# The back half of an attention pipeline moved one tile step later, with a sixth score buffer

## The chip, the cores and the metric

The kernel runs on one NeuronCore of a Trainium2 chip. The metric is the device time in microseconds; the median of the runs is what counts. Engines are named as the profile names them: PE (matmul; PEld its weight loads), DVE (vector), ACT (scalar), POOL (GpSimd), SP (issues most DMAs).

## What is computed

Attention over 4 batches, 8 heads, 576 positions and a head size of 64, in which each query keeps only its 32 largest scores; then a dense two-layer block (512 to 2048 to 512) with a hard-swish between; then a mixture of 8 experts (512 to 1024 to 512), one expert for each of 2304 tokens.

```python
scores = scale * q @ k.T                       # 4 x 8 x 576 x 576
kth = np.partition(scores, -32, axis=-1)[..., -32:-31]
attn = softmax(np.where(scores >= kth, scores, -1e9)) @ v
x = attn.transpose(0, 2, 1, 3).reshape(2304, 512)
h = x @ w_in
x = (h * np.clip(h + 3, 0, 6) / 6) @ w_out     # first block
e = argmax(x @ w_gate); p = softmax(x @ w_gate)[e]
out = p * (relu(x @ w1[e]) @ w2[e])            # experts
```

## The kernel before

**Tiles and steps.** The scores are cut into 144 tiles of 128 query rows by 576 keys (two tiles, one for each head, share a pair of heads; 16 "T" tiles hold the 64-row tails of two heads). One loop with a step counter `t` runs over the tiles (L1102 and below). In step `t` it issues the work of several tiles: scores of tile t+2 (`qk`, `sevac`), first search on tile t (`top_a`: eight MAX8 over pieces of 72, then three rounds that end in the 24 largest), thresholds, exponential and sign count of tile t-1 (`top_c`, `act_exp`, `act_sign`), second search and mask of tile t-2 (`mask`), transposes of tile t-4 (`trans`, `tevac`), the product with v and its way into the input of the first block for tile t-5 (`pv`, `xevac`, `xt`). After these, step `t` issues what the second search needs of tile t-1: the scores with the 24 largest blanked out.

**Second search.** For the first 20 tiles (`ZPE = 20`) POOL writes a mask of large negative numbers into a `z` buffer (L703, `z_pe`), and PE computes the scores a second time on top of that mask in the two PSUM banks `yps2` (`qk(t, zw)`, L630 with output yps), which the first block's second layer is not using yet. From tile 20 on DVE writes the blanked scores into a `z` buffer itself (L696, `top_z`). There are two `z` buffers. In `mask` DVE takes the 8 largest of these (L731), picks the 32nd-largest score with the sign count (`j`, L735, which reads a table in the PSUM tile `ptps`), and multiplies the exponentials by the mask (L739, read from a score buffer). `ptps` is also where the transposes (L755, L757) and the product with v (L789) land.

**Buffers.** Scores: `NSB = 3 + LA` = 5 buffers, tile t in buffer t % 5 (`LA` is 2, the lead of the scores). Exponentials: 3 pair buffers. Query tiles: 2 of each kind (`QB`); `qlast(n)` says in which step the buffer of visit n (4 tiles of a pair of heads) is free again: for the first 20 tiles after the second `qk`.

**First block.** 9 blocks of 256 tokens, 16 groups each, 144 groups. `moe_step` issues one group for each step of the loop as soon as the block's tokens are through `xt` (`blkready`): `l1` (12 matmuls, L863), `epi_a` (ACT, L869), `epi_b` (DVE, L875), `epi_c` (POOL), `l2` (6 matmuls, L894). By the loop's own count block 0 is ready in step 21 and group 0 is issued in step 22, one group a step from then on without a gap; the last step of the loop is 150, with group 128, and the remaining groups follow in a loop without attention. The weights of the first block come as 64-bit numbers and are converted in 32 pieces (`conv64`), 15 in 16 steps, from the start on; a piece has three DVE operations (L329, L336, L339), in `cvs` buffers of which there are three. `gate` transposes the first block's output (`yt`, one buffer) for the expert choice.

**Order.** Every issue sets a due time, `pr(name)`: the step's base plus 400 for each step plus an entry of the table `PRIO` (L50). The framework's scheduler orders each engine's instructions by due time among those whose inputs are already placed, allots buffers, and adds the waits. Engines run their own lists in order. Entries that matter here: `exp=-295, qk=10, pv=-40, top_c=55, mask=55, zw=60, zpe=70, prep=105, sign=175, trans=210, top8=270, l2=260, l1=310, max8=315, z=365, sevac=390, match=560`.

Of the kernel before, what the change touches and what calls it, by code (L numbers as in the profile page):

```python
# [13 lines left out]
F32 = mybir.dt.float32  # L14
# [4 lines left out]
AF = mybir.ActivationFunctionType  # L19
# [11 lines left out]
LA = 2  # L31
# [16 lines left out]
ZPE = 20  # L48
# [9 lines left out]
def attention_two_moe_kernel(  # L58
# [13 lines left out]
    PE, V, A, G, SP = nc.tensor, nc.vector, nc.scalar, nc.gpsimd, nc.sync  # L72
# [5 lines left out]
    P = 128  # L78
# [75 lines left out]
    def pr(name, least=0):  # L154
        tc.cur_priority = max(least, pr0[0] + PRIO[name])
# [72 lines left out]
    def body(cs, exact, ends=None):  # L228
# [160 lines left out]
        if not exact:  # L389
            identb.append(ap1.tile([P, P], BF16, name="identb"))  # L390
            G.tensor_copy(identb[0], ident)
        NPB, NSB, VB = 3, 3 + LA, 2

# [304 lines left out]
        def z_pe(t):  # L698
            if exact or not 0 <= t < ZPE:
                return  # L700
            pr("zw")
            zw = ap1.tile([P, S], F32, tag="z", bufs=2, name=f"z{t}").bitcast(BF16)[:, 0:S]
            G.tensor_scalar(zw, ts[t]["s"][:, 0:S], ts[t]["u"], -HUGE, op0=ALU.is_gt, op1=ALU.mult)  # L703
            qk(t, zw)

# [8 lines left out]
        def act_sign(t):  # L714
            if exact:
                return
            pr("sign")
            d = ts[t]
            jk = ap1.tile([P, S], BF16, tag="jk", bufs=1, name=f"jk{t}")
            d["sg"] = ap1.tile([P, 1], F32, tag="sg", bufs=3, name=f"sg{t}")  # L720
            A.activation(jk, d["s"][:, 0:S], AF.Sign, bias=ts[t]["u"], scale=-1.0, accum_out=d["sg"])  # L721

        def mask(t):
# [3 lines left out]
            if not exact:  # L727
                pr("max8")
                z8 = ap1.tile([P, 8], F32, tag="z8", bufs=3, name=f"z8_{t}")
                j8 = ap1.tile([P, 8, 2], F32, tag="j8", bufs=1, name=f"j8_{t}")  # L730
                V.max(z8, d["z"])  # L731
                A.activation(zall[:, t:t + 1], z8[:, 1:2], AF.Sign, bias=ts[t]["u"], scale=-1.0)
                yield
                pr("match")
                V.scalar_tensor_tensor(j8, psum_isum, d["sg"], z8.unsqueeze(2).to_broadcast([P, 8, 2]), op0=ALU.is_equal, op1=ALU.mult,  # L735
                                       accum_out=tall[:, t:t + 1])
                yield
# [171 lines left out]
        def gate(bk, tt, y):  # L909
            pr("gate")  # L910
            i = bk * (TB // P) + tt
            last = bk == NBLK - 1
            yt = (wp[0] if last else m1p).tile([P, NCC, P], F32, tag="yt", bufs=1 + last, name=f"yt{i}")
            for hf in range(0 if last else 2):
# [186 lines left out]
        cacc = 0  # L1101
        for t in range(T + 7):  # L1102
            pr0[0] = pbase + t * STEP
            loads(t)
            if t == 5:
                load_gates(ts[5]["s"])
            while vloaded[0] < NV and (vloaded[0] < VB or vlast[vloaded[0] - VB] <= t - 6):
                load_v()
            ms = moe_step()
            next(ms, None)  # L1110
            if 0 <= t - 4 < T:
                trans(t - 4)
            if 0 <= t - 1 < T:
                top_c(t - 1)
                act_exp(t - 1)
            if t + LA < T:
                ensure(t + LA)
                qk(t + LA)
            if 0 <= t - 5 < T:
                pv(t - 5)  # L1120
            if t + LA < T:
                sevac(t + LA)
            if 0 <= t - 5 < T:
                xevac(t - 5)
            xg = None
            if xtq and (xtq[0][2] < t - 5 or t >= T):
                xg = xt(*xtq.pop(0))
                next(xg)
            if 0 <= t - 4 < T:
                tevac(t - 4)  # L1130
            if xg:
# [10 lines left out]
            cacc += CRATE  # L1142
            others = [ms, mask(t - 2)]
            while cacc >= 16:
# [315 lines left out]
```

## Time and profile before

| | us |
|---|---|
| median of 3 runs | 1199.18 |
| lowest, highest | 1198.66, 1202.45 |
| the profiled execution | 1204.39 |
| its span from the first to the last instruction | 1202.5 |
| PE, PEld busy | 1118.5, 1003.8 |
| DVE busy | 940.9 |
| ACT busy | 807.6 |
| POOL busy | 458.5 |

The attention loop ends at about 880 us of the span; groups of the first block without attention fill the time to about 930 us; the experts follow. The profile's PE time is modelled: matmuls are pipelined and a busy PE need not be at its peak. Waits are idle times of an engine, put down to the event that ended them.

### The profile page before, as it was taken

To read this page: it belongs to the slowest core of one execution; us is meant where nothing else is said; L and a number is where in the kernel's file an instruction comes from. 1 tells how busy PE (TensorE), PEld (TensorE's weight loads), DVE (VectorE), ACT (ScalarE), POOL (GpSimd) and SP (SyncE) were. 2 spreads that over 40 slices of the span, in tenths; PEclk is the share of its full clock that TensorE was granted. 3 is DMA by queue.
4 is the path that set the end of the run, shared out by engine and by line. 5 is a ranking of instruction groups with operands and counts; after the bars stand their busy time and mean duration, and the time that the engine had idled before them with its cause. 6 is when DMAs were issued, how large, how long until landed. Compare 5 with 4: busy or idle time off the path is not lost.

```text
span 1202.5 us, 24061 instructions
## 1 busy us (share of the span) xinstructions
PE 1118.5 (93%) x7414; PEld 1003.8 (83%) x7414; DVE 940.9 (78%) x3853; ACT 807.6 (67%) x2082; POOL 458.5 (38%) x668
## 2 busy tenths in 40 slices
PE   5677688999999999999999999999999899999995
PEld 4566577778999989999988899999888799888885
DVE  5989989999999999998999899999641554545540
ACT  4777877778878788778778788777541353444441
POOL 5877646644332354433342432322344311222110
PEclk9668879999999999999999999999999899999998
DMA  3654456564553555754444554543486555455530
GB/s 76 189 179 142 143 171 221 162 174 125 157 134 113 151 134 142 177 135 135 118 122 126 133 147 125 152 133 110 127 271 163 176 187 179 161 176 185 160 121 31
DMA packets 184123, 179.24 MB, mean 149 GB/s; under 512 B 123629, under 2 KB 148509, under 8 KB 183984
## 3 DMA queue, kind: packets, MB, share of 16 engines
q1 hardware_dynamic: 178960, 167.24, 48.3%
q0 software_dynamic: 3872, 10.08, 2.6%
q8 instruction: 61, 1.00, 0.4%
q14 instruction: 78, 0.64, 0.2%
q10 hardware_dynamic: 1152, 0.28, 0.1%
HBM read 159.53 MB, written 18.61 MB: 148 GB/s over the span
## 4 chain that ended last, share of the span: by engine, by line
PE 71%; DVE 16%; issue 5%; ACT 4%; POOL 2%; DMA 2%; SPq 0%; POOLq 0%; ACTq 0%; DVEq 0%
PE l1ps L863 15%; PE yps L894 13%; PE ptps L789 9%; PE lp L1263 8%; PE ops L1286 8%; PE sps L630 6%; PE ptps L755 4%; DVE cd L660 2%; DVE pbuf L739 2%; DVE z L696 2%; DVE z L731 1%; PE ptps L935 1%; DVE m L666 1%; DVE cw L671 1%; PE misc L474 1%
## 5 line engine op out<-in xcount | busy, mean ns | idle before, releaser
L894 PE MATMUL yps<-wo,gh 128*128 128x512 f32 x544 | 206.7, 418 | 0.1
L298 POOL TENSOR_SCALAR gh<-gf 128x256 fp32r<-128x256 f32 x144 | 72.7, 505 | 345.2 <-PE yps L894 196.0
L660 DVE MAX8 cd<-sbuf 128x8 f32<-128x72 f32 x1152 | 187.9, 218 | 3.4 <-ACT sbuf L300 3.2
L863 PE MATMUL l1ps<-xh,wih 128*128 128x256 f32 x576 | 167.6, 291 | 4.7 <-DVE gf L875 3.1
L863 PE MATMUL l1ps<-xh,wil 128*128 128x256 f32 x576 | 164.0, 285 | 0.0
L863 PE MATMUL l1ps<-xl,wih 128*128 128x256 f32 x576 | 163.9, 285 | 0.0
L789 PE MATMUL ptps<-vn,pt 128*128 128x65 f32 (+1 forms) x1152 | 145.8, 281 | 0.0
L789 PEld LDWEIGHTS ptps<-vn,pt 128*128 128x128 f32 x1152 | 143.0, 201 | 0.0
L739 DVE SCALAR_TENSOR_TENSOR pbuf<-sbuf,tall,pbuf 128x576 f32<-128x576 f32 x144 | 136.8, 950 | 0.1
L883 POOL TENSOR_TENSOR gl<-gf,gh 128x256 fp32r<-128x256 f32 x144 | 125.5, 871 | 11.4
L863 PEld LDWEIGHTS l1ps<-xh,wih 128*128 128x128 f32 x576 | 110.4, 192 | 14.9 <-DVE gf L875 7.6
L1036 DVE TENSOR_TENSOR wl<-raw,wh 128x1024 fp32r<-128x1024 f32 x64 | 78.6, 1236 | 53.7 <-ACT wh L1035 51.6
L721 ACT ACTIVATE jk<-sbuf,uall 128x576 bf16<-128x576 f32 x144 | 111.6, 775 | 4.2 <-DVE j L735 0.9
L863 PEld LDWEIGHTS l1ps<-xl,wih 128*128 128x128 f32 x576 | 110.6, 192 | 4.2
L712 ACT ACTIVATE pbuf<-sbuf,nb 128x576 f32<-128x576 f32 x144 | 111.2, 775 | 4.1 <-PE ptps L757 0.9
L894 PEld LDWEIGHTS yps<-wo,gh 128*128 128x128 f32 x544 | 101.2, 190 | 14.8 <-POOL qh L486 0.3
L300 ACT ACTIVATE sbuf<-sps 128x576 f32<-128x576 f32 x144 | 92.9, 645 | 30.4 <-PE sps L630 16.5
L869 ACT ACTIVATE gf<-l1ps,three 128x256 f32<-128x256 f32 x144 | 67.9, 471 | 66.9 <-PE l1ps L863 55.7
L755 PE MATMUL ptps<-ident,pbuf 128*128 128x128 f32 x576 | 93.9, 286 | 19.7 <-DVE j L735 12.6
L894 PE MATMUL yps<-wo,gl 128*128 128x512 f32 x272 | 110.4, 406 | 0.6 <-POOL gl L883 0.6
L863 PEld LDWEIGHTS l1ps<-xh,wil 128*128 128x128 f32 x576 | 110.6, 192 | 0.1
L630 PE MATMUL sps<-kx,qh 128*128 128x288 f32 (+2 forms) x336 | 96.8, 319 | 14.3 <-ACT sbuf L300 10.5
(259 smaller groups left out, 2974.7 us busy)
## 6 DMA issues: line engine op xcount, KB each, us to landing
wo<-wod SPq DMA_DIRECT2D x144, 512.0 KB, 3.8
raw<-in_moe_w_dram SPq DMA_DIRECT2D x64, 512.0 KB, 4.3
vn<-in_v_dram SPq DMA_DIRECT2D x96, 128.0 KB, 2.7
rawi<-in_moe_w_in_dram SPq DMA_DIRECT2D x16, 512.0 KB, 4.0
rawo<-in_moe_w_out_dram SPq DMA_DIRECT2D x16, 512.0 KB, 4.6
wod<-wc SPq DMA_DIRECT2D x16, 512.0 KB, 5.6
qn<-in_q_dram SPq DMA_DIRECT2D x126, 64.0 KB, 2.5
yd<-y SPq DMA_DIRECT2D x18, 258.0 KB, 5.1
```

Of the source, the lines that this page charges most:

```text
L630: PE.matmul(d_, a_, b_, start=(i == 0), stop=(i == len(mm) - 1))
L660: V.max(cd[:, c, :], s[:, c * CK:(c + 1) * CK])
L712: A.activation(d["p"], d["s"], AF.Exp, bias=d["nb"], scale=SCALE)
L721: A.activation(jk, d["s"][:, 0:S], AF.Sign, bias=ts[t]["u"], scale=-1.0, accum_out=d["sg"])
L739: V.scalar_tensor_tensor(d["p"], d["s"], tall[:, t:t + 1], d["p"], op0=ALU.is_ge, op1=ALU.mult)
L755: PE.transpose(ptps[:, c * P:(c + 1) * P], pb[:, c0 + c * P:c0 + (c + 1) * P], ident)
L789: PE.matmul(d_, a_, b_, start=(i == 0), stop=(i == len(mm) - 1))
L863: PE.matmul(dst, a[:, c, fs], b_[:, c, :], start=(n == 0), stop=(n == 3 * NCC - 1))
L883: G.tensor_tensor(gl, gf, r_(gh), op=ALU.subtract)
L894: PE.matmul(acc(bk, tt), a[:, tsl], b_, start=(f == 0 and m == 0), stop=(f == NF1 - 1 and m == 2))
L1263: PE.matmul(lp, a[:, c, fs], b_[:, c, 0:w], start=(n == 0), stop=(n == 3 * NCC - 1))
L1286: PE.matmul(ops_[j][0:n], a, b_[:, ns], start=(f == 0 and i == 0), stop=(f == NF2 - 1 and i == len(ms) - 1))
```

## The change

Everything from the second search on is issued one step later with respect to the tile: exponential of tile t-2 instead of t-1, mask of t-3 instead of t-2, transposes of t-5 instead of t-4, product with v of t-6 instead of t-5. The 8 largest of the blanked scores move out of `mask` into a function of their own (`second`, tile t-3), the second scores of the first 20 tiles out of `z_pe` into `z_mm` (tile t-2); POOL's mask, the threshold, the sign count and DVE's blanked scores stay at t-1. The loop has one step more. A sixth score buffer and a fourth `sg` are added; `yt` has no buffer of its own any more, except in the last block, but shares the three of `cvs`. The table of due times stays as it is, and so do `qlast`, the two `z` buffers and the three pair buffers.

```diff
-        NPB, NSB, VB = 3, 3 + LA, 2
+        NPB, NSB, VB = 3, 4 + LA, 2
...
             G.tensor_scalar(zw, ts[t]["s"][:, 0:S], ts[t]["u"], -HUGE, op0=ALU.is_gt, op1=ALU.mult)
-            qk(t, zw)
+            ts[t]["zw"] = zw
+
+        def z_mm(t):
+            if not exact and 0 <= t < ZPE:
+                qk(t, ts[t]["zw"])
...
-            d["sg"] = ap1.tile([P, 1], F32, tag="sg", bufs=3, name=f"sg{t}")
+            d["sg"] = ap1.tile([P, 1], F32, tag="sg", bufs=4, name=f"sg{t}")
...
+        def second(t):
+            if exact or not 0 <= t < T:
+                return
+            d = ts[t]
+            pr("max8")
+            d["z8"] = ap1.tile([P, 8], F32, tag="z8", bufs=3, name=f"z8_{t}")
+            V.max(d["z8"], d["z"])
+            A.activation(zall[:, t:t + 1], d["z8"][:, 1:2], AF.Sign, bias=ts[t]["u"], scale=-1.0)
...
             if not exact:
-                pr("max8")
-                z8 = ap1.tile([P, 8], F32, tag="z8", bufs=3, name=f"z8_{t}")
+                pr("match")
                 j8 = ap1.tile([P, 8, 2], F32, tag="j8", bufs=1, name=f"j8_{t}")
-                V.max(z8, d["z"])
-                A.activation(zall[:, t:t + 1], z8[:, 1:2], AF.Sign, bias=ts[t]["u"], scale=-1.0)
-                yield
-                pr("match")
+                z8 = d["z8"]
...
-            yt = (wp[0] if last else m1p).tile([P, NCC, P], F32, tag="yt", bufs=1 + last, name=f"yt{i}")
+            yt = (wp[0] if last else m1p).tile([P, NCC, P], F32, tag="yt" if last else "cvs", bufs=2 if last else 3, name=f"yt{i}")
...
-        for t in range(T + 7):
+        for t in range(T + 8):
...
-            while vloaded[0] < NV and (vloaded[0] < VB or vlast[vloaded[0] - VB] <= t - 6):
+            while vloaded[0] < NV and (vloaded[0] < VB or vlast[vloaded[0] - VB] <= t - 7):
                 load_v()
...
-            if 0 <= t - 4 < T:
-                trans(t - 4)
+            if 0 <= t - 5 < T:
+                trans(t - 5)
             if 0 <= t - 1 < T:
                 top_c(t - 1)
-                act_exp(t - 1)
+            if 0 <= t - 2 < T:
+                act_exp(t - 2)
+            second(t - 3)
+            z_mm(t - 2)
...
-            if 0 <= t - 5 < T:
-                pv(t - 5)
+            if 0 <= t - 6 < T:
+                pv(t - 6)
...
-            if 0 <= t - 5 < T:
-                xevac(t - 5)
+            if 0 <= t - 6 < T:
+                xevac(t - 6)
             xg = None
-            if xtq and (xtq[0][2] < t - 5 or t >= T):
+            if xtq and (xtq[0][2] < t - 6 or t >= T):
...
-            if 0 <= t - 4 < T:
-                tevac(t - 4)
+            if 0 <= t - 5 < T:
+                tevac(t - 5)
...
-            others = [ms, mask(t - 2)]
+            others = [ms, mask(t - 3)]
```

## Rows read from the trace of the kernel before

**Rows 1.** The page: busy time by engine, then PE and DVE in 40 slices.
```profile
PE 1118.5 (93%) x7414; PEld 1003.8 (83%) x7414; DVE 940.9 (78%) x3853; ACT 807.6 (67%) x2082; POOL 458.5 (38%) x668
...
PE   5677688999999999999999999999999899999995
...
DVE  5989989999999999998999899999641554545540
```

**Rows 2.** Windows: from:to, length, busy us by engine (instructions), PEclk, DMA share, GB/s.
```profile
30.00:150.00 120.00, 83.69 (x464) 71.90 (x463) 112.62 (x432) 95.79 (x248) 88.84 (x69) 0.76 0.56 163
150.00:240.00 90.00, 80.23 (x504) 69.46 (x504) 86.42 (x329) 68.52 (x184) 50.47 (x66) 0.91 0.58 185
...
340.00:840.00 500.00, 495.50 (x3638) 457.49 (x3637) 465.41 (x2174) 399.28 (x1117) 170.41 (x280) 1.00 0.50 135
...
880.00:936.00 56.00, 55.37 (x355) 48.25 (x355) 18.20 (x50) 18.85 (x43) 24.82 (x41) 1.00 0.68 201
```

**Rows 3.** Waits of DVE, 0 to 30 us: total us, times, longest us.
```profile
DVE z L731 <- PE yps L630: 3.9, 2, 2.9
```

**Rows 4.** Waits of DVE, 30 to 150 us.
```profile
DVE xl L839 <- ACT xh L835: 4.1, 2, 2.6
DVE rs L802 <- PE ptps L789: 2.5, 2, 2.1
DVE cd L660 <- ACT sbuf L300: 0.7, 1, 0.7
```

**Rows 5.** Waits of PE, 30 to 150 us.
```profile
PE ptps L755 <- DVE j L735: 7.5, 4, 3.7
...
PE yps L630 <- DVE z L731: 7.1, 5, 2.1
...
PE sps L630 <- ACT qh L482: 2.8, 1, 2.8
```

**Rows 6.** Waits of PE, 150 to 240 us.
```profile
PE ptps L755 <- DVE j L735: 3.7, 5, 1.4
```

**Rows 7.** Waits of PE, 340 to 840 us: the two longest.
```profile
PE misc L449 <- POOL kd L443: 2.1, 2, 1.5
PE ptps L755 <- DVE j L735: 0.8, 2, 0.4
```

**Rows 8.** DVE by form, 30 to 240 us: busy us, mean ns, idle us before.
```profile
L739 DVE SCALAR_TENSOR_TENSOR pbuf<-sbuf,tall,pbuf 128x576 f32<-128x576 f32 x31 | 34.5, 1114 | 0.0
...
L731 DVE MAX8 z<-yps 128x8 f32<-128x576 f32 x17 | 12.6, 744 | 0.0
...
L735 DVE SCALAR_TENSOR_TENSOR j<-ptps,sg,z 128x16 f32<-128x16 f32 x31 | 6.9, 223 | 0.3 <-ACT pt L300 0.3
...
L875 DVE SCALAR_TENSOR_TENSOR gf<-gf,l1ps 128x256 f32<-128x256 f32 x12 | 4.9, 410 | 1.4 <-ACT gf L869 1.4
```

**Rows 9.** PE in order of time, 867 to 874 us: start us, us, what.
```profile
867.65 0.62 PE L755 MATMUL ptps<-ident,pbuf 128*128 128x128 f32 x4
868.11 0.27 PE L757 MATMUL ptps<-ident,pbuf 128*128 128x128 f32 x1
868.14 0.48 PE L894 MATMUL yps<-wo,gh 128*128 128x512 f32 x1
...
871.05 0.38 PE L789 MATMUL ptps<-vp,pt 128*128 128x130 f32 x2
...
872.97 0.48 PE L894 MATMUL yps<-wo,gh 128*128 128x512 f32 x1
```

**Rows 10.** Line 869, 882 to 929 us: count, ns min/median/max, first and last start us.
```profile
L869 ACT ACTIVATE gf<-l1ps,three x16: 473/474/475, 882.6 to 927.7; 128x256 f32<-128x256 f32 x16
```

**Rows 11.** All engines in order of time, 92 to 110 us, around visit 4's queries.
```profile
100.88 0.63 ACT L300 ACTIVATE sbuf<-sps 128x576 f32<-128x576 f32 x1
101.44 0.74 DVE L731 MAX8 z<-yps 128x8 f32<-128x576 f32 x1
...
102.08 0.58 ACT L482 ACTIVATE qh<-misc 128x512 fp32r<-128x512 f32 x1
...
102.24 0.30 PE L630 MATMUL yps<-z,identb 128*128 128x288 bf16 x1 [2.09 <-DVE z L731]
...
108.55 1.16 DVE L660 MAX8 cd<-sbuf 128x8 f32<-128x72 f32 x8
```

## The prediction

> **What bounds the kernel now.** I read the page first, then windows by stage, then the waits of DVE and PE in each stage, then single stretches in order of time. In [rows 1] the two lines of 40 slices show that no engine bounds the whole: DVE is near full from the second slice to two thirds of the span, PE only from about 240 us on. The windows [rows 2] put numbers on it. From 30 to 150 us DVE is busy for 112.6 of 120 us and PE for 83.7; from 150 to 240 us DVE for 86.4 of 90 and PE for 80.2. This is the stage with the conversion of the weights, and DVE sets its pace. From 340 to 840 us PE is busy for 495.5 of 500 us, DVE for 465.4: PE sets the pace, DVE is close behind. From 880 to 936 us, groups of the first block without attention, PE is busy for 55.4 of 56 us and DVE for 18.2.
>
> The waits tell what a deeper pipeline could take away. DVE's: 3.9 us at the very start for PE's second scores [rows 3], later 4.1 and 2.5 us in the chain from the product with v to the block's input [rows 4]. PE's: 7.5 us for DVE's match and 7.1 us for DVE's second search from 30 to 150 us [rows 5], 3.7 us for the match until 240 us [rows 6], and in the 500 us of the middle nothing longer than 2.1 us in all, the match at 0.8 [rows 7]. So the stage where PE is the bound has next to no waits of the kind that the change can reach, and the stage where PE waits has DVE as its bound.
>
> **The change part by part.** No instruction is added or removed. What changes is which tile's back half stands in which step.
>
> *Edges that get a step of slack:* threshold to exponential, POOL's mask to the second scores, blanked scores and sign count to the match. The only wait above that one of these ends is DVE's 3.9 us [rows 3]: the second search of tile 0 stands in DVE's list ahead of the search of tile 3 and waits for PE. It goes. But next late are the scores themselves: soon after, DVE waits 0.7 us for a score evacuation [rows 4], in the start that loads and transposes k and q. I take 0 for it; the bounds are 0 and -3.9 us.
>
> *Edges that get none:* the match waits on `ptps` together with the transposes of a tile two steps older, before and after; the second scores of tile t still need the second search of tile t-1 to have emptied `yps2`, before and after in the same step; a score buffer is still released by the mask of the step before, since the sixth buffer is eaten up by the mask's extra step; pair buffers likewise, as exponential and transposes move together. So the 7.5, 7.1 and 3.7 us [rows 5, 6] should stay: 0.
>
> *The exponential* keeps its due time of -295 in a step that is 400 later, so it is due at 105 of the old step, after the threshold at 55 and ahead of the sign count at 175, where it stands now: 0.
>
> *The early stage loses work.* When DVE reaches a given search, it has done one tile's back half less and one group less, because groups start when block 0 is through, now in step 23 instead of 22. On DVE that is 0.74 (second search) + 0.22 (match) + 1.11 (mask) + 0.41 (a group's `gf`) = 2.48 us [rows 8], in a stage in which DVE is busy for 94 to 96% of the time [rows 2]: -2.4 us. The bounds are -2.5 and 0, if scores are late instead.
>
> *The end gets that work.* The loop has one step more, and from the first group to the last the steps are in unbroken sequence, so one more group stands behind the attention. The 16 `gf` from 882.6 to 927.7 us [rows 10] are 45.1 / 15 = 3.0 us apart, and with PE busy for 55.4 of 56 us [rows 2] nothing covers it: +3.0 us. One tile's transposes and product with v move into PE-bound time too: five transposes take 868.14 - 867.65 = 0.49 us (four for the other half of the tiles, an estimated 0.39), a pair's product 872.97 - 871.05 = 1.92 us, so 0.44 + 0.96 = 1.4 us for a tile [rows 9]. Together +4.4 us; the bounds are +3.0 (the tile's share fits beside the groups) and +4.4.
>
> *Buffers whose slack shrinks.* Two `z` buffers now hold two finished tiles when the third is written. From tile 20 on writer and reader are both DVE in the right order (due at 365 and 315): 0. For the first 20 tiles POOL's mask may wait for PE, but its result is wanted a step later than before: 0. The query buffers are tighter: `qlast` still allows their preparation in the step after the next, and that is now the step of the last second scores that read them. In [rows 11] the copy of new queries (102.08 us) stands just before the second scores of tile 12 (102.24), which follow the second search at 101.44; after the change tile 11's scores stand there, and the copy must follow them, about 1.1 us later. It concerns five visits, 2 to 6. What hides it is the lead of the scores: tile 15's are evacuated at 100.88 us and searched from 108.55 us on [rows 11], 7.7 us. PE's longest wait for a query copy is 2.8 us [rows 5], less than that. I take 0; the bounds are 0 and 5 x 2.8 = 14 us, nearer to 0.
>
> *Loads and gates.* The loads of v are issued one step later, and so is the product that frees their buffers; in SP's list they move past the weight loads of one group, with a step of slack as before. The rows of `yt` in `cvs` come after all conversions by 16 steps of groups (group 15 must be done first), so three buffers where one was: 0 at the least.
>
> *The middle.* Each engine has the same operations at the same due times, those of the back half for a tile one older. A new order can cost or gain there; PE's whole idle time is 500 - 495.5 = 4.5 us [rows 2], which bounds a gain; I take the same for a loss, an estimate.
>
> Sum: -2.4 + 4.4 = **+2.0 us**. Against the profiled execution's own 1204.39 us (span 1202.5) that is 1206.4 us; this execution was 5.2 us above the median of 1199.18, so on the scale of the median **1201.2 us**.
>
> **Rivals.**
> *Faster: the waits were a shortage of buffers.* If a deeper supply lets the scheduler place matches earlier, the start's 3.9 us, the 3.7 us before 240 us, where groups already fill PE, and the 0.8 us of the middle go [rows 3, 6, 7]: 8.4 us, 1192.8 us. For it: PE does wait for DVE again and again there (5 times, [rows 6]). Against it: these waits are between operations that move together. The Trainium skill (Perfetto Trace Analysis, Optimization Strategy) says that a gap which repeats on the engine that should be saturated can mean too few buffers for the next tile. The trace agrees with it only where PE is not the saturated engine; by that rule the sum would be this rival's.
>
> *Slower: query preparation collides with the second scores.* Place: steps of tiles 3 to 21, on ACT and PE. Price 1.1 us for each of five visits, 5.5 us, so 1206.7 us, and up to 14 us, 1215.2 us. It decides as soon as the scores' lead of 7.7 us [rows 11] is used up. Against it: that lead.
>
> *It does nothing:* the scheduler orders by due time among what is ready, so it may fill the extra step with early work, and early gain and late cost cancel: 1199.2 us. Against it: PE has no room from 880 us on.
>
> **How the numbers follow.** Forecast 0.42, faster 0.22, slower 0.26, nothing 0.10. The forecast's own range is 1198 to 1204 us. The range goes from 1201.2 - 3.9 - 4.5 = 1192.8 us (start and middle at their gain) to 1201.2 + 2.4 + 4.5 = 1208.1 us, rounded up to 1208.5, which takes in both priced rivals except the slower one's far bound. A measurement of this kernel can tell about 0.3%, 3.6 us, from no change. Of the forecast's 0.42 some 0.34 lie within it and 0.08 above; of the faster rival 0.19 are below; of the slower one 0.25 above; nothing counts as same. That gives 0.19 faster, 0.48 same, 0.33 slower.
>
> **What would show it.** Right: PE busy about 55 of 56 us again behind the attention, with one group more there and its last `gf` later by about 2 us; searches around tile 34 earlier by about 2 us; DVE's 3.9 us at the start gone, and PE's waits for the match as long as now. Wrong: the middle's steps shorter or longer by more than 1% of 500 us (reordering is then the main effect); DVE waiting for score evacuations between 60 and 160 us, with PE waiting for query copies (slower rival); the waits for the match halved (faster rival).

## The result and the profile after

The changed kernel takes 1214.26 us (median of 4 runs, 1211.99 to 1216.68) against 1200.82 us of the kernel before in the same measurement: a ratio of 1.0108, interval 1.0089 to 1.0127. On a second chip it was 1219.82 us, 1.0174 [1.0152, 1.0196]. The forecast of 1201.2 us and its range up to 1208.5 us missed it: the change costs 13 us on the first chip and 19 us on the second. The profiled execution took 1211.99 us, span 1210.2 us.

The page after answers [rows 1]: busy time by engine, then PE and DVE in 40 slices.
```profile
PE 1121.7 (93%) x7414; PEld 1008.6 (83%) x7414; DVE 949.8 (78%) x3853; ACT 807.5 (67%) x2082; POOL 444.8 (37%) x668
...
PE   5577778999999999999999999999999899999995
...
DVE  4899999999999999999899899999741454445540
```
The counts of instructions are those of before, but DVE is busy for 8.9 us longer with the same 3853 instructions (940.9 us before). An engine that does the same work in more time is the first thing to follow up.

The windows of the changed kernel, those of [rows 2] (from:to, length, busy us by engine, PEclk, DMA share, GB/s):
```profile
30.00:150.00 120.00, 83.98 (x460) 71.73 (x460) 112.20 (x425) 93.81 (x242) 87.19 (x70) 0.74 0.54 163
150.00:240.00 90.00, 74.83 (x445) 66.06 (x446) 87.96 (x316) 65.52 (x176) 41.48 (x58) 0.85 0.57 178
340.00:840.00 500.00, 494.49 (x3630) 456.04 (x3629) 467.24 (x2178) 398.37 (x1115) 164.91 (x284) 1.00 0.50 135
880.00:936.00 56.00, 56.00 (x365) 49.82 (x365) 18.02 (x47) 19.10 (x41) 27.19 (x42) 1.00 0.73 228
```
From 150 to 240 us DVE is busy for longer (88.0 against 86.4 us) and finishes less (316 instructions against 329); PE loses 5.4 us of work, and its clock is granted at 0.85 instead of 0.91. Here the kernel falls behind.

To place the loss I read seven moments off each trace: when DVE begins the first search of tiles 4, 21, 36, 70 and 143, the last `gf` of the first block, and ACT's first operation of the experts. Their differences, in us:

| | to tile 4 | 4–21 | 21–36 | 36–70 | 70–143 | to last `gf` | to experts |
|---|---|---|---|---|---|---|---|
| before | 29.8 | 113.8 | 104.3 | 190.6 | 410.9 | 78.3 | 25.2 |
| before_again | 29.6 | 113.6 | 102.8 | 189.9 | 410.9 | 78.5 | 25.6 |
| changed | 33.3 | 110.5 | 109.5 | 189.9 | 411.1 | 81.1 | 25.1 |
| after_again | 33.5 | 109.7 | 108.7 | 193.9 | 415.2 | 81.3 | 25.2 |
| after_sub_later | 33.4 | 109.6 | 101.2 | 187.7 | 410.2 | 81.0 | 25.1 |
| after_pool_late | 33.2 | 110.1 | 100.9 | 194.3 | 412.2 | 81.3 | 28.4 |
| after_pool_no_reload | 33.3 | 112.9 | 101.1 | 188.9 | 410.8 | 81.4 | 26.0 |
| after_pool_late_again | 33.2 | 113.0 | 100.8 | 190.3 | 411.4 | 81.3 | 25.2 |
| after_no_reload | 33.4 | 111.2 | 108.8 | 188.8 | 410.5 | 81.5 | 28.9 |
| after_steps_back | 33.3 | 108.7 | 106.0 | 200.4 | 417.5 | 81.2 | 26.2 |
| after_sub_steps_back | 33.5 | 111.4 | 107.0 | 194.7 | 417.7 | 81.4 | 25.1 |
| before_steps_moved | 30.5 | 110.0 | 105.3 | 193.0 | 410.0 | 79.7 | 25.2 |
| before_moe_late | 29.4 | 113.1 | 102.3 | 189.2 | 411.4 | 83.9 | 29.4 |

What follows the experts' start takes 249.5 to 250.5 us in every row. The labels in the other rows are those of the experiments below. Three things stand out. The end, from the last search to the last `gf`, is 2.8 us longer in the first trace of the changed kernel than in that of before, and 2.5 to 3.2 us longer in every other version of the changed kernel. Tiles 21 to 36 are 5.2 us longer in the first pair of traces and 5.9 us in the second. Tiles 36 to 143 are as before in the first trace (601.0 against 601.5 us) and 8.3 us longer in the second, of the same program (609.1 against 600.8). The rest of this section shows where the second comes from; the third needed the experiments, and the first is taken up with the prediction.

DVE, by form, in the stretch of tiles 21 to 36: the blanking L696 (busy us, mean ns, idle before). Before, 144 to 248 us:
```profile
L696 DVE SCALAR_TENSOR_TENSOR z<-sbuf,uall 128x576 f32<-128x576 f32 x15 | 15.0, 1000 | 0.0
```
After, 144 to 253 us:
```profile
L696 DVE SCALAR_TENSOR_TENSOR z<-sbuf,uall 128x576 f32<-128x576 f32 x15 | 21.5, 1430 | 0.0
```
The same 15 operations take 6.5 us longer. One by one most take either about 0.80 us or about 1.77 us: of tiles 20 to 35, 3 are longer than 1.2 us before and 10 after. What is beside a short and a long one, in order of time on DVE and POOL (start us, us). Before:
```profile
178.72 0.74 DVE L731 MAX8 z<-z 128x8 f32<-128x576 f32 x1
178.75 0.62 POOL L298 TENSOR_SCALAR wc<-cvo 128x512 fp32r<-128x512 f32 x1 [2.23 <-DVE cvo L339]
179.38 0.80 DVE L696 SCALAR_TENSOR_TENSOR z<-sbuf,uall 128x576 f32<-128x576 f32 x1
179.46 1.85 POOL L347 TENSOR_TENSOR wc<-cvo,wc 128x512 fp32r<-128x512 f32 x1
```
After:
```profile
177.61 0.73 DVE L733 MAX8 z<-z 128x8 f32<-128x576 f32 x1
177.64 0.62 POOL L298 TENSOR_SCALAR wc<-cvo 128x512 fp32r<-128x512 f32 x1 [1.89 <-DVE cvo L339]
178.27 0.07 DVE L671 MATCH_VALUE_LOAD cw<-m,cw 128x8 f32 x1
178.33 0.20 DVE L671 MATCH_REPLACE8 cw<-m,cw 128x64 f32<-128x64 f32 x1
178.34 1.26 POOL L347 TENSOR_TENSOR wc<-cvo,wc 128x512 fp32r<-128x512 f32 x1
178.45 1.76 DVE L696 SCALAR_TENSOR_TENSOR z<-sbuf,uall 128x576 f32<-128x576 f32 x1
```
Before, the blanking begins 0.08 us ahead of POOL's subtraction (the low part of a converted weight): DVE takes 0.80 us, POOL 1.85. After, a `match_replace` of the running search stands between the second search and the blanking; the subtraction begins 0.11 us ahead, POOL takes 1.26 us and DVE 1.76. Each time the one that comes second pays. The other tiles of the changed kernel show the same. Of its 10 long blankings 9 begin behind a subtraction that is still running on POOL: 8 by 0.05 to 0.24 us behind one of a weight, one by 0.46 us behind one of a key. The four short ones that have a subtraction of a weight beside them begin 0.07 to 0.46 us ahead of it. In the tenth long one the subtraction is recorded 0.02 us later, too close to tell. The start of the subtraction is tied to DVE, too: by the copy L298 to the conversion's last operation on DVE. So the order of DVE's small operations decides who is first.

The Trainium skill (SBUF — State Buffer, the section "SBUF: two separate sides") says that DVE and GpSimd share one pair of SBUF ports, that a DVE operation with two SBUF inputs and a GpSimd operation which reads SBUF exclude each other for the whole instruction, and that the first to start gets it. The rows agree: 0.80 and 1.85 us one way, 1.76 and 1.26 the other.

### The profile page after: what moved, and what is told of

Same layout as the page of the kernel before. It is cut to its first block, busy times and chain, and to the rows that moved or that the text cites. A ratio compares the mean times of both kernels' runs of the same rounds, so it can differ in the third digit from the quotient of the medians.

```text
span 1210.2 us, 24115 instructions
## 1 busy us (share of the span) xinstructions
PE 1121.7 (93%) x7414; PEld 1008.6 (83%) x7414; DVE 949.8 (78%) x3853; ACT 807.5 (67%) x2082; POOL 444.8 (37%) x668
## 4 chain that ended last, share of the span: by engine, by line
PE 71%; DVE 16%; issue 6%; ACT 3%; POOL 2%; DMA 1%; SPq 0%; POOLq 0%; DVEq 0%; ACTq 0%
PE l1ps L872 14%; PE yps L903 13%; PE ptps L798 9%; PE lp L1275 8%; PE ops L1298 8%; PE sps L630 5%; PE ptps L764 4%; DVE cd L660 2%; DVE pbuf L748 2%; DVE z L733 2%; DVE z L696 2%; PE ptps L944 1%; DVE m L666 1%; DVE cw L671 1%; PE misc L474 1%
## 5 line engine op out<-in xcount | busy, mean ns | idle before, releaser
L298 POOL TENSOR_SCALAR gh<-gf 128x256 fp32r<-128x256 f32 x144 | 68.4, 475 | 361.3 <-PE yps L903 201.5
L798 PE MATMUL ptps<-vn,pt 128*128 128x65 f32 (+1 forms) x1152 | 142.3, 276 | 0.0
L798 PEld LDWEIGHTS ptps<-vn,pt 128*128 128x128 f32 x1152 | 139.3, 197 | 0.0
L892 POOL TENSOR_TENSOR gl<-gf,gh 128x256 fp32r<-128x256 f32 x144 | 123.8, 860 | 11.3
L1045 DVE TENSOR_TENSOR wl<-raw,wh 128x1024 fp32r<-128x1024 f32 x64 | 78.3, 1232 | 53.0 <-ACT wh L1044 52.7
L872 PEld LDWEIGHTS l1ps<-xl,wih 128*128 128x128 f32 x576 | 111.8, 194 | 4.4
L878 ACT ACTIVATE gf<-l1ps,three 128x256 f32<-128x256 f32 x144 | 68.2, 473 | 68.6 <-PE l1ps L872 58.3
L696 DVE SCALAR_TENSOR_TENSOR z<-sbuf,uall 128x576 f32<-128x576 f32 x124 | 113.4, 915 | 0.2 <-ACT uall L684 0.2
L764 PE MATMUL ptps<-ident,pbuf 128*128 128x128 f32 x576 | 95.6, 291 | 13.1 <-DVE j L744 11.3
```

The lines of the kernel that those rows point to most:

```text
L696: V.scalar_tensor_tensor(d["z"], s, d["u"], s, op0=ALU.is_le, op1=ALU.mult)
L764: PE.transpose(ptps[:, c * P:(c + 1) * P], pb[:, c0 + c * P:c0 + (c + 1) * P], ident)
L798: PE.matmul(d_, a_, b_, start=(i == 0), stop=(i == len(mm) - 1))
L872: PE.matmul(dst, a[:, c, fs], b_[:, c, :], start=(n == 0), stop=(n == 3 * NCC - 1))
L892: G.tensor_tensor(gl, gf, r_(gh), op=ALU.subtract)
```

## The experiments

Each ratio is to runs of the kernel before on the same chip. In the expectations, theory P is this collision; S, that the longer end costs all; O, that DVE's new order costs by itself; L, that late loads do; Q is told below.

**Moving one of the two.** The last DVE operation of a conversion gets a later due time, in both kernels (after_sub_later, before_sub_later):
```diff
+            tc.cur_priority += 100
             V.scalar_tensor_tensor(wb, lo, 29, wb, op0=ALU.logical_shift_right, op1=ALU.bitwise_or)
```


> The changed kernel with one due time moved: the third DVE operation of a weight conversion piece, which sets off POOL's copy and subtraction, is due 100 later. No work is left out. Theory P (a collision): in the changed kernel DVE's blanking of the scores starts about 0.1 us after POOL's subtraction has begun and then takes 1.77 instead of 0.80 us, in 10 of the 16 tiles 20 to 35; with the later subtraction all 16 take 0.8 us, which is 6 to 7 us, and the time falls from 1214 to 1206-1208 us. Theory S (the extra step itself costs it all: one more group behind the attention, a deeper pipeline to fill): the blanking may get shorter, but the time stays at 1212-1215 us.

> The kernel before with the same due time moved by 100. Theory P: it has the collision in 3 of 16 blankings, and some masks of the first 20 tiles meet the subtraction too; 3 to 6 us faster than before, 1195-1198 us. Theory S: within 2 us of before, 1199-1203 us.

The changed kernel falls to 1199.07 us, 0.9985 [0.9968, 1.0001]; the same edit to the kernel before gives 1201.47 us, 1.001 [0.9991, 1.0028]. The blankings of after_sub_later, 143 to 244 us:
```profile
L697 DVE SCALAR_TENSOR_TENSOR z<-sbuf,uall 128x576 f32<-128x576 f32 x15 | 12.5, 833 | 0.0
```
None is long any more, and tiles 21 to 36 take 101.2 us. But P misses on both sums. The changed kernel gains twice what P had expected (1206 to 1208 us): in the trace tiles 36 to 143 take 597.9 us, 3.1 less than in the first trace of the changed kernel and 11.2 less than in the second. The kernel before was to gain 3 to 6 us; its long blankings fall from three to one and tiles 21 to 36 to 101.3 us, and no gain shows in the median. The edit shifts other operations too, so alone it doesn't prove the collision.

**Taking POOL's read away.** POOL's subtraction becomes a memset, which reads nothing (after_sub_memset, before_sub_memset):
```diff
-            G.tensor_tensor(l, wf, r_(h), op=ALU.subtract)
+            G.memset(r_(l), 0.0)
```


> The changed kernel with POOL's 32 subtractions of the weight conversion (the low parts of both weights of the first block) replaced by a memset of the same tile, so the low parts are zero; POOL then reads nothing there. Theory P: the blanking takes 0.8 us in all 16 tiles and the time is at 1204-1208 us; the distance to the kernel before with the same edit is 4 to 7 us, what is left for the extra step. Theory S: that distance is still 12-14 us.

> The kernel before with the same 32 subtractions replaced by a memset (low parts of the weights zero). Theory P: 3 to 6 us faster than before, 1195-1198 us, as masks and blankings no longer meet the subtraction. Theory S: within 2 us of before.

1195.41 us, 0.9949 [0.993, 0.9968], against 1202.15 us, 1.0016 [0.9993, 1.0039]: the edit is worth over 1% to the changed kernel and nothing to the kernel before. In the changed kernel 15 blankings take 905 ns in the mean. P had expected 1204 to 1208 us, and 1195 to 1198 us for the kernel before, and misses both. The edit also gives POOL less to do (0.52 us for the memset, 1.26 for the subtraction), and the trace of the changed kernel takes 104.2 us for tiles 4 to 21, where no blanking stands yet, instead of 110.5. So this is no measure of the collisions alone.

**Only the start of the subtraction.** A small copy on POOL ahead of it, some 0.2 us, with DVE's order exactly that of the changed kernel:
```diff
             copy(CH, h, wf)
+            G.tensor_copy(l[:, 0:1, 0:128], r_(h[:, 0:1, 0:128]))
             G.tensor_tensor(l, wf, r_(h), op=ALU.subtract)
```


> The changed kernel with one small POOL instruction (a copy of 128 x 128 elements, overwritten by the subtraction) between POOL's copy and its subtraction of each of the 32 conversion pieces. DVE's order is the same instruction for instruction as in the changed kernel; POOL only begins its subtraction some tenths of a us later. Theory P (the blanking loses when the subtraction is already running): the blankings of tiles 20 to 35 fall from 1.40 to about 0.85 us and the time from 1214 to 1199-1205 us, though POOL has more to do. Theory O (what helped before was the new order of DVE's conversion work): the time stays at 1211-1216 us.

> The changed kernel with the small POOL copy ahead of the subtraction, once more. Its first profile had short blankings (0.89 us) and 100.9 us for tiles 21 to 36, but 194.3 us for tiles 36 to 70 (a query load that PE waited 2.3 us for, and then a stretch at about half the clock) and 28.4 us from the last group to the experts. Theory P: these two losses were chance, the time falls to 1200-1206 us. Theory L: they belong to this order of work, come again, and the time is 1211-1217 us.

In order of time (after_pool_late):
```profile
177.21 0.29 POOL L347 CAST wc<-wc 128x128 fp32r<-128x128 f32 x1
177.35 0.81 DVE L697 SCALAR_TENSOR_TENSOR z<-sbuf,uall 128x576 f32<-128x576 f32 x1
177.58 1.71 POOL L348 TENSOR_TENSOR wc<-cvo,wc 128x512 fp32r<-128x512 f32 x1
```
An added operation makes the blanking the first again: 2 long ones of 16, tiles 21 to 36 in 100.9 us instead of 109.5. Theory O falls, as DVE's order is untouched. But the whole time was 1215.4 us, 1.013 [1.01, 1.0161], no better than the 1.0108 of the changed kernel. On the second chip it was 1208.52 us, 1.008 [1.0057, 1.0102], where the changed kernel took 1219.82. P had expected 1199 to 1205 and 1200 to 1206 us. The collisions were gone from the stage, and 8 to 13 us of loss were still there. So P is not all.

**The other way round, in the kernel before.** A MAX8 ahead of each blanking of the first 36 tiles (before_blank_late), and as a control one behind it (before_max_behind):
```diff
+            if t < 36:
+                V.max(d["z"][:, 0:8], s[:, 0:72])
             V.scalar_tensor_tensor(d["z"], s, d["u"], s, op0=ALU.is_le, op1=ALU.mult)
```


> The kernel before with one more MAX8 over 72 values (0.14 us net) on DVE ahead of each blanking of tiles 20 to 35; its result is overwritten. 16 x 0.14 = 2.2 us of DVE work. Theory P: the blanking now starts after the subtraction has begun, takes 1.4 to 1.8 us, and the time rises by 2.2 + 6 to 12 us, to 1209-1215 us. Theory O: 2 to 3 us, 1203-1205 us.

> The control: the same MAX8 of 0.14 us behind each of those 16 blankings instead of ahead (it reads the blanked scores and goes to a tile that nobody reads). Both theories: the blankings as in the kernel before, 1201-1205 us.

Ahead: 10 long blankings of 16, tiles 21 to 36 in 111.8 us; behind: 4 and 106.5. But the medians are 1207.84, 1.0059 [1.0033, 1.0085], just under P's 1209 to 1215, and 1205.85, 1.0035 [1.0011, 1.006], just over the 1201 to 1205 expected. The collisions came as expected, the 5.3 us of the stage did not reach the median: the intervals overlap. This pair is inconclusive on the price.

**The longer end alone.** In the kernel before, one step issues no group, so that all follow a step later (before_moe_late; at the border of two blocks it starts and stops some sums of the second layer in another order, which changes that part of the computation):
```diff
-            ms = moe_step()
+            ms = moe_step() if t != 22 else iter(())
```


> The kernel before, in which the first block's groups start one step later (group 0 in step 23 instead of 22), so that one more group stands behind the attention; nothing else of the change. By the prediction's terms: +3.0 us for the group at the end and -0.4 us for its DVE share in the early stage, 1203-1204 us. If groups are worked off in idle PE time anyway: 1200-1202 us.

1207.33 us, 1.0045 [1.0016, 1.0073], 4.6 us more than before and above the 1203 to 1204 us expected. Its trace has 83.9 us to the last `gf` (78.3 before, 81.1 in the changed kernel). Counted in the traces, 25 groups begin their epilogue (`gf` on ACT) behind the start of the last search; before it is 23, in the changed kernel 24. So this edit makes the end longer by two groups, 5.6 us, and is no measure of the one group of the change. The 29.4 us to the experts hold a wait of PE of 2.45 us for the experts' gathered inputs. Theory S falls by another run: after_sub_later has the longer end of the changed kernel (81.0 us) and takes 1199.07 us.

**The same programs again**, on one chip:

> The changed kernel once more, for a second profile beside the other three of this call. Theory P (the collision in tiles 20 to 35 sets the time): 1212-1216 us, and from the search of tile 21 to that of tile 36 again 107-111 us, where the kernel before took 104 and the version with the later subtraction 101. Theory L (losses later on, where loads come late: tiles 36 to 70, and between the first block and the experts): the stage from 21 to 36 may differ, but tiles 36 to 70 or the passage to the experts are 3 us or more longer than in the version with the later subtraction (187.7 and 25.1 us).

> The kernel before once more, for a second profile. Both theories: 1199-1204 us; tiles 21 to 36 in 102-105 us, tiles 36 to 70 in 188-191 us, 78.3 us from the last tile's search to the last group, 25 us from there to the experts.

> The changed kernel with the later subtraction once more. Both theories: 1197-1202 us, the blankings short, tiles 36 to 70 in 188 us. If it comes out above 1205 us, its first time was chance and neither theory holds.

1219.82 us, 1201.76 us (1.0011 [0.9997, 1.0024]) and 1200.93 us (1.0006 [0.9991, 1.0021]). Long blankings: 10, 3 and 0 of 16, as the first time; a program's collisions repeat. What did not repeat is in tiles 36 to 143 of the changed kernel: 601.0 us, then 609.1.

**Where those 8.3 us are.** The waits of PE in the changed kernel, 340 to 840 us, the two longest ([rows 7] are those before):
```profile
PE misc L474 <- DMA qn<-in_q_dram: 2.1, 2, 1.1
PE ptps L970 <- DVE oh L969: 0.9, 1, 0.9
```
PE waits for a load of queries, twice; before it never did in these 500 us, though it waited for a key [rows 7]. PE in order of time, query transposes (L474) and key transposes (L449) between 418 and 436 us. Before:
```profile
420.35 0.38 PE L474 MATMUL misc<-ident,qn 128*128 128x128 f32 x2
424.43 0.66 PE L449 MATMUL misc<-ident,kd 128*128 128x128 f32 x4 [1.49 <-POOL kd L443]
...
433.41 0.38 PE L474 MATMUL misc<-ident,qn 128*128 128x128 f32 x2
```
After:
```profile
423.99 0.38 PE L474 MATMUL misc<-ident,qn 128*128 128x128 f32 x2
428.91 0.42 PE L474 MATMUL misc<-ident,qn 128*128 128x128 f32 x2 [1.15 <-DMA qn<-in_q_dram]
```
The two transposes stand 13.1 us apart before and 4.9 us after. There is one buffer for unprepared queries, so the second load can be issued only when the first transposes are through. What places the preparations is one line that the diff does not touch: `pj = t < T and xg is None and pstart(t + LA)`. A preparation is begun only in a step that transposes no attention outputs; these transposes moved by a step, from odd to even ones, and with them the choice of what is prepared when. At tile 66, before begins key 9, the changed kernel one step later query 23.

In after_again the same place reads, PE in order of time first, then PE by windows (from:to, length, PE busy, PEclk, DMA share, GB/s):
```profile
428.03 0.66 PE L474 MATMUL misc<-ident,qn 128*128 128x128 f32 x2 [1.65 <-DMA qn<-in_q_dram]
```
The windows around it:
```profile
420.00:425.00 5.00, 5.00 (x37) 1.00 1.01 188
425.00:430.00 5.00, 3.32 (x22) 0.89 0.81 165
430.00:435.00 5.00, 5.00 (x20) 0.50 0.10 22
435.00:440.00 5.00, 5.00 (x34) 0.92 0.38 105
```
While the load is under way the DMA engines are full; PE waits for 1.65 us, and then its granted clock falls to 0.50, the lower of its two levels (1.2 GHz), for 20 matmuls in 5 us instead of 34 to 39. At 620 us the same happens after a wait of 1.4 us. These two are the stages 36–70 and 70–143, 4.0 and 4.1 us above the first trace, whose waits of 1.15 and 0.94 us left the clock at 1.00. Over all traces, 22 waits of PE above 0.9 us stand at these two places. Behind 9 of them, of 1.4 to 2.9 us, the clock fell; behind 13, of 0.9 to 3.2 us, it did not. The length of the wait alone does not tell which, and the 1.5 us that one expectation below names is no border: the clock fell behind 1.40 us and stayed behind 3.17. Six of the 22 waits, all for a key, stand in versions of the kernel before, and one of these (1.89 us, in before_moe_late) has a fall behind it.

So theory L became theory Q: the preparations moved, PE waits for a load at two places, and the clock makes the wait dear.

**Moving the preparations.** The changed kernel with the preparations on the steps of before (after_steps_back), the same on top of after_sub_later (after_sub_steps_back), and the kernel before with those of the changed kernel (before_steps_moved):
```diff
-            pj = t < T and xg is None and pstart(t + LA)
+            hold = bool(xtq and xtq[0][2] < t - 5)
+            pj = t < T and not hold and pstart(t + LA)
```
```diff
-            pj = t < T and xg is None and pstart(t + LA)
+            pj = t < T and not xgl[0] and pstart(t + LA)
+            xgl[0] = xg is not None
```


> Edit: in the changed kernel a step begins a key or query preparation unless the attention outputs are due to be transposed in the NEXT step (before: unless they are transposed in this one), which puts the preparations on the steps they have in the kernel before (of 120 steps every one agrees). Theory Q (the change moved the preparations by a step, two query preparations then come 5 us apart on one query buffer, TensorE waits for the load of the second, and its granted clock falls behind the longer of these waits): no TensorE wait for the query load at tiles 70 and 103 (2.1 and 3.0 us in the two traces of the changed kernel), no stretch under full clock there, tiles 36 to 143 at 598 to 601 us (changed kernel: 601.0 and 609.1). Theory P (collision of VectorE's blanking with GpSimd's subtraction) says nothing of these, and expects the blankings and tiles 21 to 36 as they were, 109 us. Both together: some 1207 us. If the steps of the preparations are beside the point: 1212 to 1219.

> Edit: the changed kernel with the third conversion operation due 100 later (after_sub_later: no collision), and with the preparations on the steps of the kernel before. Theory Q: the short waits for the query load of after_sub_later (0.7 to 1.0 us in sum) go, and nothing else; 1197 to 1200 us, a ratio of 0.997 to 1.0. If the steps of the preparations in the changed kernel were better for the rest: 1201 to 1205 us.

> Edit: the kernel before, with the preparations of keys and queries on the steps that they have in the changed kernel (a step begins none when the step ahead of it transposed attention outputs), the score pipeline as it was. Theory Q: TensorE waits for the query load appear (1 to 4 us in sum in tiles 36 to 143, none in the kernel before), with or without a fall of the granted clock behind them; 1202 to 1209 us. If the waits come from the deeper pipeline and not from the steps of the preparations: no such wait, 1200 to 1202 us.

1220.55 us, 1.0137 [1.0108, 1.0165]; 1220.8 us, 1.0139 [1.0102, 1.0176]; 1205.48 us, 1.0028 [1.0012, 1.0045]. The first two miss by 13 us and more; the third lies in Q's 1202 to 1209 us, but without the waits that Q expected. The wait for queries did go, but another took its place; waits of PE in after_steps_back, 400 to 640 us:
```profile
PE misc L449 <- POOL kd L443: 4.8, 2, 2.9
```
Now it is the load of a key (through POOL's conversion, 2.1 us in all before), with the clock at 0.76 and 0.51 in a window of 5 us behind the two; after_sub_steps_back has waits of 3.2 and 2.1 us there, with one fall of the clock. And moving the steps alone, with the old pipeline, brings no wait for queries. So the steps choose which load PE meets too early. What makes the wait long is not shown; a deeper pipeline is not needed for it, as before_moe_late has 1.89 us. The part of Q that says the steps are at fault falls; the part on the waits and the clock is left to test.

These two waits are not the whole loss of the two kernels. In after_steps_back the granted clock is at 0.63 from 246 to 260 us as well. And after_sub_steps_back takes 107.0 us for tiles 21 to 36 with 1 long blanking of 16. Waits of DVE, 144 to 252 us:
```profile
DVE xl L849 <- ACT xh L845: 5.5, 4, 3.0
DVE gf L885 <- ACT gf L879: 3.0, 3, 1.8
```
So this stage can lose as much without collisions. It measures them only between versions in which DVE works in the same order, as in the changed kernel and after_pool_late.

**Taking the load away.** The two loads that PE waits for are left out (the scores of visits 23 and 35 are then those of other queries), and every instruction of PE, DVE and POOL keeps its place. Without and with the small copy on POOL (after_no_reload, after_pool_no_reload), and after_pool_late once more for company (recorded as after_pool_steps_back, but with no step moved):
```diff
-                qraw[n] = ap1.tile([P, 2, 2, 2, D], F32, tag="qn", bufs=1, name=f"qn{n}")
+                qraw[n] = qkeep[0] if n in (23, 35) else ap1.tile([P, 2, 2, 2, D], F32, tag="qn", bufs=1, name=f"qn{n}"); qkeep[0] = qraw[n]
                 nf = w // P
-                for h in range(2):
+                for h in range(0 if n in (23, 35) else 2):
```


> Edit: in the changed kernel the queries of visits 23 and 35 are not loaded; the preparation transposes the queries of visit 22 and 34 once more from the buffer where they lie (so the scores of these two visits are those of other queries). The order of instructions on TensorE, VectorE and GpSimd is that of the changed kernel, only those loads are gone. These are the two visits whose load TensorE waits for (1.15 and 0.94 us in one trace of the changed kernel, 1.65 and 1.4 us in the other, where the granted clock then fell to half for some 10 us each). Theory Q (the rest of the loss is these waits and the clock behind them): no wait there, no stretch under full clock between 300 and 860 us, tiles 36 to 70 at 188 to 189 us and 70 to 143 at 410 us (with the waits alone 189.9 and 411.1, with the clock's falls 193.9 and 415.2); the collisions stay; median 1205 to 1209 us. If the clock falls for another reason: 1213 to 1220 us as before.

> Edit: the same two loads left out (and the same two visits with other queries) in the changed kernel with GpSimd's subtraction some 0.2 us later (after_pool_late), which has hardly any collision. Theories P and Q together account for all of the loss: 1199 to 1203 us (after_pool_late: 1208.5, 1210.2 and 1215.4). If the loss of after_pool_late has another cause: 1207 to 1215 us.

> Repeat of the changed kernel with GpSimd's subtraction some 0.2 us later (after_pool_late), as company of the other three on one chip. Theory Q: TensorE waits 2.5 to 4.2 us for the query load again (two waits), and where the longest is over 1.5 us the clock falls to about half for some 10 us behind it; 1205 to 1216 us. If the losses were chance: no wait, 1199 to 1202 us.

after_pool_no_reload: 1205.27 us, 1.0025 [1.0011, 1.004], between the 1199 to 1203 us expected if P and Q are all and the 1207 to 1215 if not, where after_pool_late had 1.008 and 1.013 (and 1210.18 us in one more run, again with a wait of 1.64 us and the clock at 0.50 behind it). Its windows of PE at the two places:
```profile
400.00:440.00 40.00, 40.00 (x296) 1.00 0.58 144
...
600.00:640.00 40.00, 40.00 (x289) 1.00 0.48 120
```
No wait, no fall of the clock; stages 36–70 and 70–143 are at 188.9 and 410.8 us, no longer than before. after_no_reload has these stages right too (188.8 and 410.5), but its time is 1215.05 us, 1.0102 [1.0078, 1.0126], against 1205 to 1209 expected, a miss: what remains in its trace against before_again is 6.0 us in tiles 21 to 36, 3.0 at the end, 3.3 in the passage to the experts and 1.4 up to tile 21, less 1.5 in between. The expectation had left out the end and that passage, where PE waits 1.8 us for the experts' gathered inputs and its clock falls once more behind that.

The last pair ran on one chip, and differs by the copy of 0.29 us alone: 1215.05 (1212.21 to 1218.32) against 1205.27 us (1204.05 to 1208.15), 9.8 us apart. Their traces are 8.7 us apart: 7.7 us in tiles 21 to 36, where the collisions are; 2.9 us in the passage to the experts, with the wait just told; and -1.9 us in the rest. So the collisions' price in the stage is 7.7 us, and it is not shown that the rest of the 9.8 is theirs. The same two programs with their loads, after_again and after_pool_late_again on one chip, are 11.3 us apart: in the traces 7.9 us in tiles 21 to 36 and 7.4 in tiles 36 to 143, where the second waits for 1.38 and 1.13 us at the two places and its clock stays at 1.00.

## Why the prediction was wrong

*The `z` buffers: "writer and reader are both DVE in the right order (due at 365 and 315): 0".* This is the step that failed first. The order of these two was right; what stands beside them on POOL was not looked at. The rows to see it by were there: [rows 8] has the mask, another operation with two SBUF inputs, at a mean of 1114 ns, and the trace of before has blankings of 0.80 and 1.77 us. In its place: 10 collisions instead of 3; tiles 21 to 36 are 5.2 us longer in the first trace than before, and 7.7 us longer than in the version of the last pair that hardly collides. Why the scheduler puts the `match_replace` ahead of the blanking now was not settled.

*The middle: "each engine has the same operations at the same due times", 0 with bounds of 4.5 us.* False in one place, the preparations, which go by the steps of `xt`. Tiles 36 to 143 took 0.5 us less than before in one execution and 8.3 us more in another. The bound came from PE's idle time, which says what could be gained; a loss through the clock is not in it. That the steps alone cause it is refuted; what makes these waits long, and why the clock falls behind some of them, stays open. The rows above show only that the load is under way while the DMA engines are full.

*The start wait, "It goes", price 0.* It grows: waits of DVE in the changed kernel, 0 to 30 us ([rows 3] before):
```profile
DVE z L733 <- PE yps L630: 3.5, 1, 3.5
```
And 30 to 150 us, where [rows 4] have no such wait:
```profile
DVE z L733 <- PE yps L630: 5.8, 3, 2.6
```
DVE waits 9.2 us in all for PE's second scores, four times up to 48 us, where it waited 3.9 us before. Why is not settled. The first tiles lose 3.5 us; in the first trace they are won back by tile 21 (143.9 us against 143.6), other versions of the changed kernel, but for the one with the memset, reach it at 142.0 to 146.3 us.

*The early stage, -2.4 us, bounds -2.5 and 0.* Not to be seen: the changed kernel reaches tile 21 0.3 us later than before and tile 36 5.4 us later (253.3 against 247.9 us). In after_sub_later, after_pool_late and their repeats, with two long blankings of 16 at most, tile 36 is reached at 244.2 to 247.6 us, against 246.0 and 247.9 before: from a gain of 3.7 us to a loss of 1.6, so whether the term is there below the collisions is not settled.

*The waits for the match, 7.5 us, "should stay".* They did, and grew. Waits of PE in the changed kernel, 30 to 150 us ([rows 5] before):
```profile
PE ptps L764 <- DVE j L744: 10.0, 4, 3.6
PE yps L630 <- DVE z L733: 7.2, 8, 2.0
...
PE sps L630 <- ACT qh L482: 2.7, 3, 1.1
```
From 150 to 240 us the wait for the match [rows 6] is gone, and another is at its place:
```profile
PE l1ps L872 <- DVE gf L884: 9.3, 6, 2.5
```
In part this is DVE's lost time arriving at PE, as `gf` stands in DVE's list among the blankings: without collisions the wait is 1.8 us in after_sub_later (144 to 252 us), but still 7.4 and 5.1 us in the two traces of after_pool_late (150 to 240 us).

*The end, +4.4 us with a lower bound of +3.0.* Right in the main, and the lower bound was the better value: 2.8 us, one group. From the start of the last search 24 groups follow instead of 23. But the extra one does not stand behind all of the attention, where the prediction had it: from PE's last product with v to the last `gf` there are 18 groups in 54.9 us, before 18 in 54.8. The groups of the changed kernel (line L878, 880 to 940 us; [rows 10] before, in a shorter window):
```profile
L878 ACT ACTIVATE gf<-l1ps,three x18: 474/474/477, 884.0 to 935.4; 128x256 f32<-128x256 f32 x18
```
They are 51.4 / 17 = 3.0 us apart, as before, and PE is busy for 56.0 of 56 us. The tile's share of 1.4 us did not add to it.

*The rivals.* The slower one had the right sign and a wrong mechanism: PE's waits for query copies are 2.7 us as before. The faster one, a shortage of buffers, found no support: the waits it would have taken away stayed. With the collisions and the two late loads out of the way (after_pool_no_reload) the ratio is 1.0025, 3 us, near the forecast's +2.0; with the collisions out by another edit (after_sub_later) 0.9985 and 1.0006. So the deeper pipeline by itself is worth about nothing, as the sum said, and the sum missed what the reordering set off. That the two agree is partly luck: the start's wait grew, and the early gain is not settled. No version here beats the kernel before with all of its work done.

## What to carry to other kernels

When a change moves operations of DVE, look up what POOL does at that time: where starts lie within 0.1 us of each other, a `match_replace` in between decides who waits, here 1 us each time for DVE. Read the conditions by which helper work is placed, also those that the diff does not touch: what is keyed to a step moves with it. And a wait of PE in a stretch where it is full costs more than its length if the clock follows it, and costs it in some executions only: repeat the trace before you explain the difference. An edit made to test one cause can move other work as well (after_sub_steps_back): compare versions in which the engine in question keeps its order.

## What the runs showed of the hardware

Blanking and subtraction, 0.80 and 1.26 us where they come first, take 1.76 and 1.85 us in the rows above where they come second. A copy of 0.29 us added on POOL took 7.7 us off the stage where they meet, and that kernel was 9.8 us faster. And PE's granted clock fell from 1.00 to 0.50 behind waits of 1.4 and 1.65 us of an engine that was otherwise full, and these two stages took 4.1 and 4.0 us more than in another execution of the same program, where the waits were 0.94 and 1.15 us and the clock stayed. Over all traces it fell behind 9 of 22 such waits.
